# Empty-tile rows of a head's weighted sums added after the fourth key tile instead of after the sixth

## The chip, the cores and the metric

One Trainium2 chip, one core. The metric is device time in microseconds (us) of one execution. Engines: PE (TensorE, matmuls), DVE (VectorE), ACT (ScalarE), POOL (GpSimd), SP (SyncE, which here issues nearly all DMAs, in order).

## What is computed

Clustered attention over 2 batches x 8 heads of 768 tokens and 64 channels, and then two feed-forward layers on 1536 tokens of 512 channels. A query sees the keys of its own cluster only:

```python
q_assign = argmax(einsum('bhsd,hcd->bhsc', q_n, c_n)); k_assign = ...   # 16 clusters
mask = q_assign[:, :, :, None] == k_assign[:, :, None, :]
scores = np.where(mask, scale * (q @ k.T), -1e9)
attn = exp(scores - max); attn = attn / (sum(attn) + 1e-9)
x = (attn @ v)                                  # to [1536, 512]
h = x @ w_in;  x = softplus(h) @ w_out          # first layer, d_ff 2048
h = x @ w_in2; out = leaky_relu(h, 0.01) @ w_out2
```

A query whose cluster has no key gets equal scores everywhere, so its output is the mean of v. The kernel has a mend for this case: a few extra rows ("empty" rows) which are multiplied with sums over v and added to the head's weighted sums.

## The kernel before

The 16 heads (2 x 8) are worked through one after the other, overlapped. A head's 768 tokens are 6 tiles of 128 (C = 6). Line numbers are those of the profile.

For each head: q and k come in (L273, L274), are split into f16 high and low parts (L293 to L295) and transposed by a DMA (L297, tile t). 24 small matmuls (L306, tile as) and a few DVE operations give the cluster of each token (L319 to L325, tile oh); ACT writes these behind the channels of tile nq (L328, L329), and a second DMA transpose (L331) makes tile **tq** from nq. Then 12 score matmuls (L345) with a DVE maximum each (L352, tile mm) give the largest score of each query; DVE (L359, L361, tile dg), six small matmuls (L366) and ACT (L374) write these maxima, with the empty marks, into rows 96 to 127 of the same tile tq. Then for each of the six tiles of keys (kt = 0 to 5), emit_s2 makes scores (L392, L393, two banks), ACT takes exponentials (L399, tile p), POOL the low part (L401, tile pl), and emit_pv adds p times v to the head's sums in tile **x**, one PSUM bank: 6 matmuls each on L428, L429 and L433. In heads 0 to 7 one of the six key tiles is multiplied in f32 instead (L415) and has no pl. emit_sv makes the sums over v (L439, L440, DVE L445, tile svr). emit_empty, six matmuls on L451, multiplies rows 96 to 127 of tq with svr and adds them to x. emit_norm (DVE L470, L471, L473, ACT L475, POOL L476) reads x and normalises.

Tile tq has 4 buffers in heads 0 to 7 and 3 later: the transpose that fills the tq of head 15 can start when the last reader of the tq of head 12 is done, and likewise 14 behind 11 and 13 behind 10. The last reader of a tq in the program is emit_empty. Tile x has one buffer.

Beside the heads run the weights of the feed-forward layer: DMA loads (L153, tile st, two buffers), decoded by DVE (L140, L143, L146) and split by ACT and DVE (L162, L163). From head 8 on the first layer of the feed-forward fills in: groups of 12 matmuls (L697, one output tile each, read by ACT in L520, L521), later L710 with 48 per output tile; the first quarter of the tokens uses Abs, Relu, Exp, Ln on ACT, the others the softplus function of ACT's tables (L509, L510). After the heads come the rest of the first layer and the second layer (L562).

The order on each engine is not written out. The program emits steps with a priority (at_pri), and a list scheduler that simulates the machine places all of them; each engine then runs its list in order, with waits on semaphores where data or a buffer come from another engine. emit_s2 and emit_pv of key tile j of head h have priority h + j/6; the last emit_pv, and before the change emit_empty, have h + 1; a smaller number goes first.

Of the kernel before, what the change touches and what calls it, by code (L numbers as in the profile page):

```python
# [43 lines left out]

FF_PRI, FF_STEP, FF_RATE = 8, 0.25, 0.75

W_FREE, W_FROM, W_TO, W_PER = 4, 8, 10, 5
W_PRI = ((0, 0.5), (17, 0.3))
W2_STEPS = 88
# [7 lines left out]
def attn_moe_kernel(  # L57
# [13 lines left out]
    V, S, G, PE = nc.vector, nc.scalar, nc.gpsimd, nc.tensor  # L71
    B, H, SEQ, D = q.shape
    NCL = cen.shape[1]
    DM, DFF = w_in1.shape
    C = SEQ // 128
# [201 lines left out]
    def load_v(h):  # L277
        b, hh = divmod(h, H)
        vv = v32s[h % V_BUFS][:, :, 0:D]
        nc.sync.dma_start(out=vv, in_=v[b, hh].rearrange("(p c) d -> p c d", c=C))  # L280
        v_t[h] = vv

    def split_v(h):
        vv, v2 = v_t.pop(h), v2s[h % V_BUFS]
        S.copy(out=v2[:, :, D:2 * D], in_=vv)
        ENG[by_group(VLO, h)].tensor_tensor(out=v2[:, :, 0:D], in0=vv, in1=v2[:, :, D:2 * D], op=ALU.subtract)
# [50 lines left out]
    MR = 96  # L337
    KS2 = 128
# [15 lines left out]
    def emit_m(h):  # L354

        dg = dgs[h % len(dgs)]
        diag = dg.rearrange("p (c s) -> p c s", s=129)
        m = diag[:, :, MR:MR + 1]
        mark[h] = V.reduce_max(out=m, in_=mms[h % 2], axis=AX)  # L359
        empty = diag[:, :, MR + C:MR + 3 * C].rearrange("p c (t s) -> p c t s", s=C)[:, :, :, 0]  # L360
        V.tensor_scalar(out=empty, in0=m.to_broadcast([128, C, 2]), scalar1=-65504.0, scalar2=None, op0=ALU.is_equal)  # L361
        t = tp2[h][0]
        for j in range(2):
            bank = ring("s2", h)
            for c in range(3 * j, 3 * j + 3):
                PE.matmul(  # L366
                    out=bank[0:KS2, (c % 3) * 128:(c % 3 + 1) * 128],
                    lhsT=dg[:, c * 128:(c + 1) * 128],
                    rhs=ident,
                    start=True,  # L370
                    stop=True,
                )
            o = bank[MR:KS2, 0:3 * 128].rearrange("p (c r) -> p c r", c=3)
            S.copy(out=t[MR:KS2, 3 * j:3 * j + 3, :], in_=o)  # L374
        tpq[h] = t
# [28 lines left out]
    XW = D + 1  # L404

    def emit_pv(h, kt):
        v2 = v2s[h % V_BUFS]
        if kt == 0:
            x_t[h] = px.tile([128, 512], F32, tag="x", name="x")
        xps = x_t[h]  # L410
        p, pb, pl = p_t.pop((h, kt))
        if pl is None:
            pf = p.rearrange("p a r -> p (a r)")
            for c in range(C):
                PE.matmul(  # L415
                    out=xps[:, c * XW:(c + 1) * XW],
                    lhsT=pf[:, c * 128:(c + 1) * 128],
                    rhs=v32s[h % V_BUFS][:, kt, :],
                    start=(kt == 0 and c == 0),
                    stop=False,  # L420
                )
            return
        pb = pb.rearrange("p a r -> p (a r)")
        pl = pl.rearrange("p a r -> p (a r)")
        for c in range(C):
            cs = slice(c * 128, (c + 1) * 128)
            o = xps[:, c * XW:(c + 1) * XW]
            PE.matmul(out=o, lhsT=pb[:, cs], rhs=v2[:, kt, D:2 * D + 1], start=(kt == 0 and c == 0), stop=False)  # L428
            PE.matmul(out=o[:, 0:D], lhsT=pb[:, cs], rhs=v2[:, kt, 0:D], start=False, stop=False)  # L429
        for c in range(C):  # L430
            cs = slice(c * 128, (c + 1) * 128)
            o = xps[:, c * XW:(c + 1) * XW]
            PE.matmul(out=o, lhsT=pl[:, cs], rhs=v2[:, kt, D:2 * D + 1], start=False, stop=False)  # L433

    def emit_sv(h):
        v2 = v2s[h % V_BUFS]
        o = ring("as")[:, 0:XW]
        for kt in range(C):
            PE.matmul(out=o, lhsT=ones, rhs=v2[:, kt, D:2 * D + 1], start=(kt == 0), stop=False)  # L439
            PE.matmul(out=o[:, 0:D], lhsT=ones, rhs=v2[:, kt, 0:D], start=False, stop=(kt == C - 1))  # L440
        q4 = slice(MR, 128)
        h16 = atile([128, XW], F16, "h16", h)
        r = atile([128, XW], F16, "svr", h)
        S.copy(out=h16[q4], in_=o[q4])
        V.scalar_tensor_tensor(out=r[q4], in0=h16[q4], scalar=sel[q4], in1=o[q4], op0=ALU.mult, op1=ALU.add)  # L445
        svs[h] = r

    def emit_empty(h):
        t, r, xps = tpq[h], svs.pop(h), x_t[h]
        for c in range(C):  # L450
            PE.matmul(out=xps[:, c * XW:(c + 1) * XW], lhsT=t[MR:KS2, c, :], rhs=r[MR:KS2, :], start=False, stop=(c == C - 1))  # L451

    def emit_out(b, hh, xn):
        nc.sync.dma_start_transpose(
            out=xt[b][:, hh // 2].rearrange("p n (c r) -> p (n c) r", c=C), in_=xn.rearrange("p n c d -> p (n c d)")
        )
# [268 lines left out]
    def behind_tk(h):  # L725
        return tc.issue_after(tki[h].ins) if h in tki else nullcontext()

    @contextmanager
    def at_pri(x):
        old = tc.cur_priority  # L730
        tc.cur_priority = pri(x)
        yield
        tc.cur_priority = old
# [8 lines left out]
    with at_pri(-9):  # L742
# [6 lines left out]
            out=ss[:, 1:2], in0=ss[:, 0:1], scalar1=ss[:, 2:3], scalar2=ss[:, 1:2], op0=ALU.mult, op1=ALU.add  # L749
# [19 lines left out]
    for v2 in v2s:  # L769
# [3 lines left out]
        out=ident, in_=ones, pattern=[[1, 128]], compare_op=ALU.is_equal, fill=0.0, base=0, channel_multiplier=-1  # L773
# [4 lines left out]
    for j in range(NCL):  # L778
# [4 lines left out]
        out=sel, in_=sel, pattern=[[0, 1]], compare_op=ALU.is_ge, fill=0.0, base=-MR - 2 * C, channel_multiplier=1  # L783
# [9 lines left out]
    def w_step():  # L793
        w0, wr = W_PRI[cnt["w"] >= 34]
        with at_pri(w0 + wr * (cnt["w"] % 34)):
            if convs:
                n = cnt["w"] - 1
                g = -1 if n < W_FREE else int(W_FROM + (W_TO - W_FROM) * (n - W_FREE) / (32 - W_FREE))
                g = min(g, max(mark, default=-1), 15)
                bank = n < 2 * KDM * DFF // 512  # L800
                if g >= 0:
                    with tc.issue_after(mark[g].ins):
                        convs.pop(0)(bank)
                else:
                    convs.pop(0)(bank)
            if wq:
                with behind_tk(wtie["h"]):
                    convs.append(wq.pop(0)())
        cnt["w"] += 1
# [86 lines left out]
    def chain(h):  # L896
        if h < NH:
            with at_pri(h - LEAD_SPLIT):
                split(h)
            with at_pri(h - LEAD_ASSIGN):  # L900
                assign_mm(h)
                assign_el(h)
            with at_pri(h - LEAD_MAX):
                for c in range(C):
                    emit_s1(h, c)
            if h + 2 < NH:
                with at_pri(h - LEAD_LOAD):
                    load(h + 2)

    def moe_steps(n):  # L910
        st["credit"] += n
        while st["credit"] >= 1.0:
            with at_pri(FF_PRI + cnt["m"] * FF_STEP):
                next(ff, None)
            st["credit"] -= 1.0
# [5 lines left out]
    for h in range(NH):  # L921
        with at_pri(h - LEAD_M):
            emit_m(h)
        chain(h + AHEAD)
        wtie["h"] = h + 2
        with at_pri(h):
            if h + 1 < NH:
                split_v(h + 1)
            if h + 2 < NH:
                with behind_tk(h + 2):  # L930
                    load_v(h + 2)
            emit_sv(h)
            if h in outs_t:
                with behind_tk(h + 2):
                    emit_out(*outs_t.pop(h))
        for j in range(C):
            with at_pri(h + j / 6):
                emit_s2(h, j)
                if j:
                    emit_pv(h, j - 1)  # L940
            if h < H - 1 and (j + h * C) % W_PER == 0:
                w_step()
            if h > H or (h == H and j > 0):
                moe_steps(FF_RATE)
            if h == H and j == 0:
                open_late()
        with at_pri(h + 1):
            emit_pv(h, C - 1)
            emit_empty(h)
        with at_pri(h + 1 - LEAD_NORM):  # L950
            emit_norm(h)
    bctx.close()
# [48 lines left out]
```

## Time and profile before

| what | us |
|---|---|
| median of 3 runs | 734.06 (734.0 to 735.52) |
| profiled execution, its own time | 732.15 |
| its span, first to last instruction | 730.4 |
| PE busy in the span | 677.0 (93%) |
| DVE, ACT, POOL busy | 517.3, 410.9, 402.5 |

Heads run from about 12 us to 315 us of the span. From there to the end PE works through the feed-forward with hardly an idle moment. A reader should ask where PE is idle before 315 us, and which engine or queue ended each of these idle stretches. In timeline rows the columns are start, length, engine, line, operation, count, and in brackets the idle time of the engine just before with what ended it; matmuls overlap in their pipe, so the pace of PE is the distance between starts.

### The profile page before, as it was taken

To read this page: it belongs to the slowest core of one execution; us is meant where nothing else is said; L and a number is where in the kernel's file an instruction comes from. 1 tells how busy PE (TensorE), PEld (TensorE's weight loads), DVE (VectorE), ACT (ScalarE), POOL (GpSimd) and SP (SyncE) were. 2 spreads that over 40 slices of the span, in tenths; PEclk is the share of its full clock that TensorE was granted. 3 is DMA by queue.
4 is the path that set the end of the run, shared out by engine and by line. 5 is a ranking of instruction groups with operands and counts; after the bars stand their busy time and mean duration, and the time that the engine had idled before them with its cause. 6 is when DMAs were issued, how large, how long until landed. Compare 5 with 4: busy or idle time off the path is not lost. (4 is left out here: it accounts for less than half of the span.)

```text
span 730.4 us, 18968 instructions
## 1 busy us (share of the span) xinstructions
PE 677.0 (93%) x7584; PEld 506.7 (69%) x7584; DVE 517.3 (71%) x1167; ACT 410.9 (56%) x1087; POOL 402.5 (55%) x494
## 2 busy tenths in 40 slices
PE   1798899998889899999999999999999999999997
PEld 1367677665656566656666566558999999999996
DVE  4797798998898782069787867965585757575545
ACT  5476666768878753355245425526555555565553
POOL 6387777778888864303324233325556465565653
PEclk9999999999999999999999999999999999999999
DMA  8985966766565632013322355787000000000000
GB/s 204 221 173 113 181 136 122 170 123 173 129 161 152 141 116 53 2 35 103 110 93 82 108 175 193 235 304 261 3 31 2 30 2 7 27 2 31 2 31 30
DMA packets 104521, 77.87 MB, mean 107 GB/s; under 512 B 78320, under 2 KB 92656, under 8 KB 104432
## 3 DMA queue, kind: packets, MB, share of 16 engines
q1 hardware_dynamic: 104288, 76.40, 40.4%
q8 instruction: 59, 0.97, 0.5%
q14 instruction: 30, 0.25, 0.1%
q10 hardware_dynamic: 144, 0.26, 0.1%
HBM read 50.36 MB, written 10.49 MB: 83 GB/s over the span
## 5 line engine op out<-in xcount | busy, mean ns | idle before, releaser
L401 POOL TENSOR_TENSOR pl<-p 128x768 f16<-128x768 f32 x88 | 128.3, 1468 | 56.3 <-ACT p L399 36.0
L352 DVE TENSOR_REDUCE mm<-s 128x1 f32<-128x384 f32 x190 | 100.6, 548 | 19.3 <-PE s L345 16.7
L562 PEld LDWEIGHTS <-w_in2h 128*128 128x128 f16 x1344 | 98.2, 98 | 5.3 <-issue 0.7
L570 DVE TENSOR_TENSOR gl<-r,gh 128x384 f16<-128x384 f32 (+1 forms) x96 | 63.2, 659 | 50.0 <-ACT gh L608 49.3
L697 PE MATMUL m<-xt,w_inh 128*128 128x384 f16 x512 | 93.8, 326 | 4.2 <-ACT rl L521 3.4
L399 ACT ACTIVATE p<-s 128x384 f32<-128x384 f32 x160 | 74.2, 492 | 30.9 <-PE s L393 28.3
L710 PE MATMUL m<-g_l,w_outh 128*128 128x384 f16 x256 | 83.4, 326 | 2.0 <-DVE g_l L511 1.9
L710 PE MATMUL m<-g_h,w_outh 128*128 128x384 f16 x256 | 83.5, 326 | 0.0
L710 PE MATMUL m<-g_h,w_outl 128*128 128x384 f16 x256 | 83.3, 326 | 0.0
L570 POOL TENSOR_TENSOR r<-r,r 128x128 f32<-128x128 f32 x95 | 47.8, 520 | 55.5 <-ACT r L600 55.2
L697 PEld LDWEIGHTS <-w_inh 128*128 128x128 f16 x512 | 49.7, 98 | 38.7 <-issue 6.1
L608 ACT CAST gh<-r 128x384 f16<-128x384 f32 (+1 forms) x96 | 54.2, 565 | 36.6 <-POOL r L570 33.6
L710 PEld LDWEIGHTS <-w_outh 128*128 128x128 f16 x512 | 49.8, 98 | 32.5
L345 PE MATMUL s<-tq 128*128 128x384 f16 x190 | 62.0, 345 | 9.3 <-DMA tq<-nq 4.5
L562 PEld LDWEIGHTS <-gh 128*128 128x128 f16 x672 | 60.5, 98 | 6.4 <-issue 1.1
L200 POOL TENSOR_TENSOR wd<-wd 128x256 f32<-128x256 f32 x32 | 29.3, 925 | 53.9 <-DVE sg L194 39.2
L562 PE MATMUL i<-xt,w_in2h 128*128 128x128 f16 x576 | 57.2, 219 | 0.1
L392 PE MATMUL s<-t 128*128 128x384 f16 x160 | 53.2, 333 | 3.1 <-ACT p L399 2.3
L393 PE MATMUL s<-tq 128*128 128x384 f16 x160 | 53.2, 333 | 1.6 <-ACT tq L374 1.6
L562 PE MATMUL i<-sh,w_in2h 128*128 128x128 f16 x384 | 53.5, 219 | 0.4 <-ACT r L600 0.4
L562 PE MATMUL i<-sl,w_in2h 128*128 128x128 f16 x384 | 53.5, 219 | 0.0
L562 PE MATMUL i<-sh,w_in2l 128*128 128x128 f16 x384 | 53.4, 219 | 0.0
(145 smaller groups left out, 1861.1 us busy)
## 6 DMA issues: line engine op xcount, KB each, us to landing
st<-in_moe_w_in_dram SPq DMA_DIRECT2D x32, 512.0 KB, 4.6
st<-in_moe_w_out_dram SPq DMA_DIRECT2D x32, 512.0 KB, 3.7
kept<-sg SPq DMA_DIRECT2D x16, 256.0 KB, 2.8
qk<-in_q_dram SPq DMA_DIRECT2D x16, 192.0 KB, 3.5
qk<-in_k_dram SPq DMA_DIRECT2D x16, 192.0 KB, 3.7
v<-in_v_dram SPq DMA_DIRECT2D x16, 192.0 KB, 4.7
kept<-sg SPq DMA_DIRECT2D x24, 128.0 KB, 2.7
out_dram<-ob SPq DMA_DIRECT2D x11, 256.0 KB, 2.0
```

The lines of the kernel that those rows point to most:

```text
L200: G.tensor_tensor(out=out, in0=in0, in1=in1, op=ALU.subtract)
L345: PE.matmul(out=o, lhsT=t[:, c, :], rhs=tk[:, 3 * j:3 * j + 3, :], start=True, stop=True,)
L352: V.reduce_max(out=mms[h % 2][:, c, j:j + 1], in_=bank[:, 0:3 * 128], axis=AX)
L392: PE.matmul(out=o, lhsT=t1[:, kt, 1, :], rhs=t1[:, 3 * j:3 * j + 3, 0, :], start=True, stop=False)
L393: PE.matmul(out=o, lhsT=t2[:, kt, :], rhs=tqh[:, 3 * j:3 * j + 3, :], start=False, stop=True)
L399: S.activation(out=p[:, j, :], in_=sp, func=AF.Exp, scale=scale)
L401: G.tensor_tensor(out=pl, in0=p, in1=pb, op=ALU.subtract)
L562: one = PE.matmul(out=bank, lhsT=w_, rhs=x_, start=(first and i == 0), stop=(i == len(ops) - 1), skip_group_check=True)
L570: eng.tensor_tensor(out=out, in0=in0, in1=in1, op=op)
L608: S.copy(out=gh[:, lo:hi], in_=r[:, lo:hi])
L697: PE.matmul(out=hp, lhsT=w_, rhs=x_, start=(i == 0), stop=(i == len(ops) - 1))
L710: PE.matmul(out=yp, lhsT=w_[:, kk, ms], rhs=g_[:, kk, :], start=(n == 0), stop=(n == 3 * KFF - 1))
```

## The change

emit_empty is called behind emit_pv of key tile 3 (when j is 4), at priority h + 4/6, instead of behind emit_pv of key tile 5 at h + 1. The stop flag of the accumulation moves from the last empty matmul to the last matmul of emit_pv. No operation is added or removed in the source; since the scheduler places everything anew, the lists of all engines differ from the end of head 0 on.

```diff
+EMPTY_AT = 4
@@ emit_pv, f32 key tile
-                    stop=False,
+                    stop=(kt == C - 1 and c == C - 1),
@@ emit_pv, low parts
-            PE.matmul(out=o, lhsT=pl[:, cs], rhs=v2[:, kt, D:2 * D + 1], start=False, stop=False)
+            PE.matmul(
+                out=o, lhsT=pl[:, cs], rhs=v2[:, kt, D:2 * D + 1], start=False, stop=(kt == C - 1 and c == C - 1)
+            )
@@ emit_empty
-            PE.matmul(out=xps[:, c * XW:(c + 1) * XW], lhsT=t[MR:KS2, c, :], rhs=r[MR:KS2, :], start=False, stop=(c == C - 1))
+            PE.matmul(out=xps[:, c * XW:(c + 1) * XW], lhsT=t[MR:KS2, c, :], rhs=r[MR:KS2, :], start=False, stop=False)
@@ loop over heads
                 emit_s2(h, j)
                 if j:
                     emit_pv(h, j - 1)
+                if j == EMPTY_AT:
+                    emit_empty(h)
...
         with at_pri(h + 1):
             emit_pv(h, C - 1)
-            emit_empty(h)
```

Three places of the new order follow. In each the numbers behind a name tell buffers apart, and a line of "..." stands for matmuls of the same kind and for weight loads. After the change the lines stand one to three further down (L451 is L454, L433 is L434, L697 is L700).

**PE, from the empty rows of head 12 (x_4678, tq_3659) to the first score matmul of head 15 (s1_4942, on tq_4940).** Before:

```order
L433 MATMUL x_4678<-v2_0_89,pl_4824 128x65
...
L451 MATMUL x_4678<-svr_4641,tq_3659 128x65
...
L393 MATMUL s2_5113<-tq_4085 128x384
...
L697 MATMUL m_4365<-xt0_83,w_inh_79 128x384
...
L428 MATMUL x_5033<-v2_1_90,p_4999 128x65
...
L433 MATMUL x_5033<-v2_1_90,pl_5000 128x65
L345 LDWEIGHTS tq_4940
L345 MATMUL s1_4942<-tq_4940 128x384
```

After:

```order
L434 MATMUL x_4678<-v2_0_89,pl_4739 128x65
...
L454 MATMUL x_4678<-svr_4641,tq_3659 128x65
...
L429 MATMUL x_4678<-v2_0_89,p_4781 128x65
...
L394 MATMUL s2_5005<-tq_4085 128x384
...
L700 MATMUL m_4277<-xt0_83,w_inh_79 128x384
...
L394 MATMUL s2_5028<-tq_4085 128x384
...
L434 MATMUL x_4678<-v2_0_89,pl_4782 128x65
...
L429 MATMUL x_4678<-v2_0_89,p_4829 128x65
...
L346 MATMUL s1_4942<-tq_4940 128x384
```

The empty rows come two key tiles of head 12 earlier; between them and the score matmuls of head 15 stand, besides the empty rows, 4 score matmuls, 12 of L697, 12 of L428 and L429, and 5 of L433 before, and 8 score matmuls, 12 of L700, 24 of L429 and L430, and 6 of L434 after.

**PE, from the empty rows of head 11 (x_4199, tq_3204) to the first score matmul of head 14 (s1_4588, on tq_4586).** Before:

```order
L433 MATMUL x_4199<-v2_2_91,pl_4396 128x65
...
L451 MATMUL x_4199<-svr_4143,tq_3204 128x65
...
L393 MATMUL s2_4744<-tq_3659 128x384
...
L697 MATMUL m_4158<-xt0_83,w_inh_79 128x384
...
L428 MATMUL x_4678<-v2_0_89,p_4644 128x65
...
L345 MATMUL s1_4588<-tq_4586 128x384
```

After:

```order
L434 MATMUL x_4199<-v2_2_91,pl_4308 128x65
...
L454 MATMUL x_4199<-svr_4143,tq_3204 128x65
...
L429 MATMUL x_4199<-v2_2_91,p_4336 128x65
...
L394 MATMUL s2_4673<-tq_3659 128x384
...
L434 MATMUL x_4199<-v2_2_91,pl_4337 128x65
...
L429 MATMUL x_4199<-v2_2_91,p_4401 128x65
...
L442 MATMUL as_4981<-v2_1_90,ones_99 128x65
...
L346 MATMUL s1_4588<-tq_4586 128x384
```

Here the group of 12 feed-forward matmuls (L697) between the two is gone: there stand 4 score matmuls, 24 of L429 and L430, 6 of L434 and 12 of L442 and L443.

**ACT, at the last exponentials of head 15 and the first softplus (L509, L512 after).** Before:

```order
L399 ACTIVATE p<-s_5699 128x384
L714 ACTIVATE xt_83<-m 128x384
L399 ACTIVATE p<-s_5741 128x384
L399 ACTIVATE p<-s_5745 128x384
L509 ACT_TABLE_LOAD
L509 ACTIVATE g_h<-m 128x384
L510 ACTIVATE mr<-m 128x384
```

After:

```order
L400 ACTIVATE p<-s_5699 128x384
L512 ACT_TABLE_LOAD
L512 ACTIVATE g_h<-m 128x384
L513 ACTIVATE mr<-m 128x384
L400 ACT_TABLE_LOAD
L400 ACTIVATE p<-s_5747 128x384
L400 ACTIVATE p<-s_5751 128x384
L512 ACT_TABLE_LOAD
```

The last two exponentials now stand behind the first softplus, and two more table loads are in the list.

## Rows read from the trace of the kernel before

**Rows 1.** Page, busy time, share of the span and instructions of each engine.

```profile
PE 677.0 (93%) x7584; PEld 506.7 (69%) x7584; DVE 517.3 (71%) x1167; ACT 410.9 (56%) x1087; POOL 402.5 (55%) x494
```

**Rows 2.** Stretches: length, busy time of each engine, granted clock, DMA share, GB/s.

```profile
core 0: us, PE busy (x) PEld busy (x) DVE busy (x) ACT busy (x) POOL busy (x), PEclk, DMA share, GB/s
...
30.00:50.00 20.00, 18.01 (x197) 12.32 (x196) 16.29 (x37) 14.49 (x36) 12.68 (x11) 1.00 1.04 231
50.00:165.00 115.00, 105.36 (x1573) 78.48 (x1571) 99.13 (x238) 77.78 (x192) 86.59 (x73) 1.00 0.68 137
165.00:250.00 85.00, 73.92 (x910) 49.26 (x908) 72.92 (x150) 70.16 (x173) 72.36 (x65) 1.00 0.61 149
```

**Rows 3.** Waits of PE, 35 to 320 us: total us, times, longest.

```profile
PE s L345 <- DVE mm L352: 3.9, 9, 0.9
PE m L697 <- ACT rl L521: 3.4, 8, 0.7
...
PE s L345 <- DMA tq<-nq: 2.3, 2, 1.9
```

**Rows 4.** Waits of the SP queue, 30 to 250 us.

```profile
SPq L331 <- PE x L451: 28.2, 8, 8.0
SPq L153 <- DVE wcp L146: 21.2, 7, 5.6
```

**Rows 5.** Timeline, PE, head 11's empty rows to head 14's scores.

```profile
225.41 0.35 PE L433 MATMUL x<-v,pl 128*128 128x65 f16 x6
225.69 0.35 PE L451 MATMUL x<-svr,tq 32*128 32x65 f16 x6
225.98 0.34 PE L392 MATMUL s<-t 128*128 128x384 f16 x1
...
226.48 0.33 PE L393 MATMUL s<-tq 128*128 128x384 f16 x1
227.43 1.46 PE L697 MATMUL m<-xt,w_inh 128*128 128x384 f16 x8 [0.63 <-ACT rl L521]
...
229.38 0.19 PE L428 MATMUL x<-v,p 128*128 128x65 f16 x1
...
229.86 0.50 PE L345 MATMUL s<-tq 128*128 128x384 f16 x2
```

**Rows 6.** Timeline, SP queue, the last two transposes into tq and what follows.

```profile
226.08 1.42 SPq L331 DMA_TRANSPOSE tq<-nq  x1
...
228.59 14.27 SPq L153 DMA_DIRECT2D st<-in_moe_w_out_dram  x4
244.72 1.46 SPq L331 DMA_TRANSPOSE tq<-nq  x1
```

**Rows 7.** Line L331: from issue to landing.

```profile
DMA to landing us min/median/max: 3.6/3.9/5.4
```

**Rows 8.** Timeline, PE, head 12's empty rows and head 15's first scores.

```profile
244.29 0.35 PE L451 MATMUL x<-svr,tq 32*128 32x65 f16 x6
...
250.18 0.50 PE L345 MATMUL s<-tq 128*128 128x384 f16 x2 [1.92 <-DMA tq<-nq]
```

**Rows 9.** Stretches around that wait.

```profile
248.27:250.18 1.91, 0.00 (x0) 0.00 (x0) 0.54 (x1) 0.81 (x2) 0.95 (x2) 1.00 1.28 84
...
250.70:254.10 3.40, 3.40 (x39) 2.37 (x36) 1.66 (x4) 2.27 (x6) 3.24 (x3) 0.50 0.88 238
```

**Rows 10.** Timeline, PE, the two next longest idle times after 30 us.

```profile
33.10 0.48 PE L393 MATMUL m<-tq 128*128 128x384 f16 x1 [1.73 <-ACT tq L374]
...
61.34 0.32 PE L393 MATMUL s<-tq 128*128 128x384 f16 x1 [1.40 <-ACT tq L374]
```

**Rows 11.** Timeline, DVE and PE, around 167 to 172 us.

```profile
166.97 0.69 DVE L140 TENSOR_SCALAR wcp<-st 128x512 int32<-128x512 int32 x1 [1.68 <-DMA st<-in_moe_w_in_dram]
...
170.34 0.32 PE L345 MATMUL s<-tq 128*128 128x384 f16 x1 [0.75 <-DVE mm L352]
171.25 0.32 PE L345 MATMUL s<-tq 128*128 128x384 f16 x1 [0.59 <-DVE mm L352]
```

**Rows 12.** Timeline, ACT, last exponential and first softplus.

```profile
308.48 0.49 ACT L399 ACTIVATE p<-s 128x384 f32<-128x384 f32 x1 [1.45 <-PE s L393]
308.99 1.28 ACT L509 ACT_TABLE_LOAD   x1
310.29 0.49 ACT L509 ACTIVATE g_h<-m 128x384 f16<-128x384 f32 x1
310.67 0.48 ACT L510 ACTIVATE mr<-m 128x384 f32<-128x384 f32 x1
```

**Rows 13.** Page, costliest groups: POOL's low parts (busy, mean ns, idle before).

```profile
L401 POOL TENSOR_TENSOR pl<-p 128x768 f16<-128x768 f32 x88 | 128.3, 1468 | 56.3 <-ACT p L399 36.0
```

## Prediction, made before the changed kernel ran

> **What bounds the kernel now.** I read the page's busy shares first: PE is busy for 677.0 us of a 730.4 us span, far ahead of DVE [rows 1]. From 315 us on, past the heads, the feed-forward keeps PE busy, so a microsecond that PE idles while the heads run is a microsecond at the end. The stretches show how much there is: PE lacks 115.00 - 105.36 = 9.6 us between 50 and 165 us, and 85.00 - 73.92 = 11.1 us between 165 and 250 us [rows 2]. PE's matmuls stay the same 7584, so the change can only move these idle microseconds, and the time at a lower clock.
>
> The waits of PE name many small causes, none over 4 us in all [rows 3]. The longest single one after 30 us is 1.92 us at 250.18, on the transpose into tq [rows 8]. The SP queue tells where that comes from: L331 stood 28.2 us, in 8 waits, behind the empty rows L451, the last reader of the tq whose buffer it fills [rows 4]. Head 15 shows the chain: L451 at 244.29, the transpose issued at 244.72, the score matmul at 250.18 [rows 6, 8]. So the empty rows matter little as work and much as the release of a buffer.
>
> **What the change does, part by part.**
>
> *The empty rows themselves.* Six take 225.98 - 225.69 = 0.29 us of PE [rows 5]. They are moved, not removed: 0 for PE. They no longer stand between the last low parts and the norm, but the norm waits in DVE's list anyway; I count nothing there, and at most 16 x 0.29 = 4.6 us if every head's end stood on PE's path, which the waits contradict: none of PE's larger ones is on x [rows 3].
>
> *Release of tq.* The new order puts the empty rows two key tiles earlier, and the last score matmuls on that tq (key tile 5) stand before them, so the release does move. But the scheduler has moved the readers of the next tq forward too, so what counts is the PE work between release and reader. Paces from the rows: 0.29 for six empty rows, 0.66 for four score matmuls (225.98 to 226.48 is three), 12 of L697 in 229.38 - 227.43 = 1.95, 12 of L428 and L429 in 0.38 to 0.48 (229.38 to 229.86), six of L433 in 0.28 [rows 5]; the 12 sums over v cost about as much as 12 of L428 and L429. The need, from the start of the empty rows to the reader, is 0.4 to issue [rows 5, 6] plus 3.9 median, 5.4 at most [rows 7]: 4.3, or 5.9.
>
> - Head 15: before, 0.29 + 0.66 + 1.95 + 0.38 + 0.2 = 3.5 us of work against 5.9 in reality; waited 1.92, the rest were small gaps. After, 0.29 + 0.38 + 0.66 + 1.95 + 0.66 + 0.28 + 0.38 = 4.6 us: the wait falls to 5.9 - 4.6 = 1.3, or to none at the median landing. I take the middle, 0.65: a gain of **1.3**. Behind the 1.92 us of idle time, PE ran at half its granted clock, 1.2 instead of 2.4 GHz, for 3.40 us of solid matmuls [rows 9]; that cost 1.7 us. Idle times of 1.73 and 1.40 us [rows 10] were not followed by a lower clock: it reads 1.00 in both stretches [rows 2]. So a wait of 0.65 gives the **1.7** back. Together -3.0, bounds -3.6 (no wait) and -0.6 (wait of 1.3 and the clock falls all the same).
> - Head 13: 0.3 us of wait, the other one of the two [rows 3], goes: after, 4.8 us of work by the same count. **-0.3**.
> - Head 14: before, the reader came 229.86 - 225.69 = 4.17 after the empty rows [rows 5], at the landing. In the new order the group of 12 feed-forward matmuls is gone from between: 0.29 + 0.38 + 0.66 + 0.28 + 0.38 + 0.38 = 2.4 us of work. The wait is 4.2 - 2.4 = 1.8 us, and nothing stands before the reader that PE could do instead. **+1.7**, bounds 0 (other waits fill it) and +3.5 (1.8 and a clock fall; 1.8 lies between the 1.73 that was not followed by one and the 1.92 that was; nearer to 1.73, so I count none).
> - Heads 4 to 10 have 15 us and more of PE work between release and reader in either order: 0.
>
> *The feed-forward groups.* A group of L697 waits for ACT to read the bank of the group before. PE's waits on this are 3.4 us in 8 [rows 3]. Before the one of 0.63 [rows 5] some 2.9 us of work stood between two groups, so 3.5 was needed there. In the new order this pair has only six low parts, 4 score matmuls and 3 of L346 between it, 0.28 + 0.66 + 3 x 0.163 = 1.4 us: a wait of 2.1 if ACT is as laden with exponentials as before, and of 0.63 if it is not. I take the middle, 1.4, in place of 0.63: **+0.7**, bounds 0 and +2.0 with another pair that comes closer.
>
> *What stands behind L331 in the SP queue.* Loads of weights follow it. One arrived late at 166.97 and held DVE for 1.68 us, and PE then waited 0.75 and 0.59 us for maxima [rows 11]. An earlier release lets that load go earlier: **-0.7**, half of the 1.34, bounds -1.34 and 0.
>
> *ACT's two extra table loads.* The first softplus now stands before the last two exponentials. ACT needs 1.28 + 0.38 + 0.48 [rows 12], another 1.28 and 0.87 for the exponentials, 4.3 us from the group's end, then POOL 1.47 for the low part [rows 13]: 5.8. PE has 5.2 us of work in its list until it needs that (20 of L697, 4 score matmuls, empty rows, 24 of L429 and L430, 12 of L434). **+0.7**, bounds 0 and 2.6 (both loads in full).
>
> The page "ScalarE: Activation LUTs" of the Trainium skill (What ACT_TABLE_LOAD costs) puts a switch of set at about 2.66 us with the drain, twice the load. In the trace the load ends at 310.27 and the next operation starts at 310.29 after an exponential that ended 0.02 before the load [rows 12], so no drain is seen and the measurement decides. By the page this term would be +3.4 and the whole +1.8.
>
> **Sum.** -3.0 - 0.3 + 1.7 + 0.7 - 0.7 + 0.7 = -0.9 us on the profiled execution's own 732.15 (span 730.4 and 1.75 around it): 731.2. The median of the runs stands 1.9 above the profiled one, so 734.06 - 0.9 = **733.1**.
>
> **The rivals.**
>
> 1. *Faster: the SP queue was the brake.* If the 28.2 us of waiting in the queue [rows 4] held more than those two readers, then score maxima, exponentials and weights all come earlier, and PE's waits on mm and tq shrink too: 3.9 on mm [rows 3] and the 1.40 [rows 10]. Half of these, 2.6, and head 14's 1.7 filled by them: -0.9 - 2.6 - 1.7 = -5.2, 728.9; with half of that 731. For it: the sheer size of the queue's wait. Against: an earlier reader was put into the list at once, so the slack is spent already.
>
> 2. *Slower: the loads ahead of the transpose take the release's place.* Before L331 of head 15 stand four weight loads, which left between 228.59 and 242.86, each held until DVE had decoded an earlier one [rows 4]; L331 itself left at 244.72 [rows 6]. If the release comes some 5 us earlier, at 239.5, the fourth load at 242.9 holds the transpose. Then the reader waits 242.9 + 3.9 less 239.2 + 4.6, 3.0 us, and the clock falls: +1.1 and 0 in place of -1.3 and -1.7, in all +3.2, 737.3. With head 14's wait drawing a clock fall as well it is 739. It decides at whether DVE's decode before that load ends earlier than the empty rows of head 12. In the new list this decode stands before the maxima's step (L359) of head 14, and PE's matmuls on that (L366) before the empty rows of head 12, so I think it does, barely.
>
> 3. *No effect: the release isn't early in time*, since the fourth key tile's low parts come late from POOL (1.47 us each [rows 13]) and the scheduler spends what it gains. Then only the reshuffle remains, within 1 us either way: 733 to 735.
>
> All lists differ from the end of head 0 on, and the small waits, some 18 us in all, are dealt anew; I allow 2 us either way for that around every case.
>
> **How the numbers follow.** The forecast with rival 3: 0.37 to come out within 0.2% (1.5 us, about what a measurement of this kernel can tell from no change). Rival 1, and the forecast's own better end: faster by more, 0.36. Rival 2, head 14's clock fall, or the extra tables and groups at their upper bounds: slower by more, 0.27. The range reaches from rival 1 at 729.5 to rival 2 at 738.0; below and above I leave one in ten each. The likeliest case's own range is 732 to 735.5.
>
> **What would show it.** Right: the transposes of heads 13 to 15 leave the SP queue at L454 of heads 10 to 12 and two key tiles before the heads' ends; an idle PE of 1 to 2 us before head 14's first L346; under 1.3 us before head 15's; clock 1.00 there; three table loads about the last exponentials with less than 1 us of PE idle. Wrong: PE idle in 50 to 250 us below 16 us or above 24 (20.7 now [rows 2]); the release of head 15's tq at a weight load instead of L454; a second stretch at half clock.

## The result, and the profile after

The changed kernel takes **739.38 us** (median of 7 runs, 736.42 to 742.18) against 734.06 (7 runs, 732.03 to 737.14) of the kernel before on the same chip: a ratio of 1.0073, interval 1.0050 to 1.0096. It is slower; I had forecast 733.1 and a range up to 738.0. The profiled execution took 740.92, its span is 739.2.

Lines of after are those of before plus 1 for the scores (L345 is L346), plus 3 from the sums over v on (L439 is L442, L451 is L454, L697 is L700). The page, busy times as in [rows 1], and its row of the granted clock in 40 slices:

```profile
PE 684.1 (93%) x7584; PEld 510.1 (69%) x7584; DVE 517.2 (70%) x1167; ACT 414.3 (56%) x1089; POOL 402.2 (54%) x494
...
PEclk9998999999998999999999999999999999999999
```

PE is busy for 7.1 us more with the same 7584 matmuls, and idle for 55.1 us against 53.4. Most of the difference of the two profiled executions is therefore slower matmuls, not waiting. The stretches of [rows 2], and four short ones in which the clock is at its lower level (1.2 instead of 2.4 GHz); columns as in [rows 2]:

```profile
50.00:165.00 115.00, 103.92 (x1485) 77.52 (x1483) 95.77 (x223) 74.50 (x186) 83.06 (x68) 0.96 0.63 135
165.00:250.00 85.00, 76.90 (x920) 50.64 (x919) 70.54 (x155) 67.26 (x165) 68.37 (x62) 0.94 0.58 133
```

```profile
56.60:63.40 6.80, 6.80 (x75) 6.29 (x71) 3.14 (x8) 3.80 (x9) 4.25 (x5) 0.50 0.80 196
152.20:155.60 3.40, 3.21 (x50) 2.87 (x50) 3.40 (x10) 1.38 (x3) 2.64 (x3) 0.50 0.61 179
206.80:210.20 3.40, 3.40 (x17) 1.70 (x14) 3.19 (x8) 2.04 (x6) 1.99 (x2) 0.50 1.04 204
230.70:237.50 6.80, 6.01 (x19) 2.87 (x20) 2.89 (x6) 3.41 (x8) 0.99 (x1) 0.50 0.62 184
```

These four are 20.4 us long; behind its start before had one of 3.4 [rows 9]. The other 17 us at half speed are worth 8.5 at most, about the difference of the two spans, 8.8. But this split belongs to the two profiles and not to the kernels: e4 below has after's order on PE and the same time, yet its profile has only 10.2 us at the lower level behind the start, and PE idle for 57.2 us. How much of the 5 us the clock holds, and how much idle time, stays open. Nor can the granted clocks of all runs settle it, since they miss the start: in both kernels PE begins at the lower level (a score matmul takes 0.48 to 0.53 us instead of 0.33) and leaves it only at about 39 us in before and 36 us in after, where the granted clock reads 1.00 all the time. The last section shows this.

Three places that the prediction spoke of. First head 14's start on PE, which answers [rows 5]: the feed-forward group between empty rows and scores is gone, and two pauses stand there, with slow matmuls (0.53 instead of 0.33 us) behind them. Then the SP queue, which answers [rows 6], and head 15's first scores, which answer [rows 8]:

```profile
226.31 0.35 PE L454 MATMUL x<-svr,tq 32*128 32x65 f16 x6
...
229.59 0.19 PE L442 MATMUL as<-v,ones 128*128 128x65 f16 x1 [1.26 <-DVE oh L326]
...
231.49 0.82 PE L346 MATMUL s<-tq 128*128 128x384 f16 x2 [1.37 <-DMA tq<-nq]
232.10 0.53 PE L393 MATMUL s<-t 128*128 128x384 f16 x1
```

```profile
226.69 1.43 SPq L332 DMA_TRANSPOSE tq<-nq  x1
228.17 0.89 SPq L281 DMA_DIRECT2D v<-in_v_dram  x1
229.17 19.72 SPq L154 DMA_DIRECT2D st<-in_moe_w_out_dram  x4
249.00 2.48 SPq L332 DMA_TRANSPOSE tq<-nq  x1
```

```profile
248.11 0.35 PE L454 MATMUL x<-svr,tq 32*128 32x65 f16 x6
...
254.11 0.50 PE L346 MATMUL s<-tq 128*128 128x384 f16 x2 [0.67 <-DMA tq<-nq]
```

The waits of PE (35 to 320 us) and of the SP queue (30 to 250 us), as in [rows 3, 4]:

```profile
PE as L307 <- DMA t<-n: 4.7, 5, 1.6
PE s L346 <- DVE mm L353: 3.9, 5, 1.3
...
PE s L346 <- DMA tq<-nq: 2.2, 3, 1.4
...
PE m L700 <- ACT rl L524: 1.8, 4, 0.5
```

```profile
SPq L154 <- DVE wcp L147: 39.0, 10, 8.0
...
SPq L332 <- PE x L454: 4.0, 3, 1.6
```

The transposes' wait on the empty rows fell from 28.2 us to 4.0, as the change means it to. Yet PE waits for tq as long as before, 2.2 us against 2.3. That is the riddle. What grew is PE's wait on the transpose of k (tile t); before had

```profile
PE as L306 <- DMA t<-n: 2.8, 4, 1.2
```

### The profile page after: what moved, and what is told of

Read it like the earlier page. It is cut to its first block, busy times and chain, and to the rows that moved or that the text cites. A ratio compares the mean times of both kernels' runs of the same rounds, so it can differ in the third digit from the quotient of the medians.

```text
span 739.2 us, 18973 instructions
## 1 busy us (share of the span) xinstructions
PE 684.1 (93%) x7584; PEld 510.1 (69%) x7584; DVE 517.2 (70%) x1167; ACT 414.3 (56%) x1089; POOL 402.2 (54%) x494
## 5 line engine op out<-in xcount | busy, mean ns | idle before, releaser
L700 PE MATMUL m<-xt,w_inh 128*128 128x384 f16 x512 | 97.0, 332 | 3.0 <-ACT rl L524 1.8
L700 PEld LDWEIGHTS <-w_inh 128*128 128x128 f16 x512 | 50.3, 99 | 37.4 <-issue 5.3
L346 PE MATMUL s<-tq 128*128 128x384 f16 x190 | 62.8, 348 | 9.9 <-DMA tq<-nq 4.8
L565 PE MATMUL i<-xt,w_in2h 128*128 128x128 f16 x576 | 57.2, 219 | 0.1
L565 PE MATMUL i<-sh,w_in2l 128*128 128x128 f16 x384 | 53.4, 219 | 0.0
```

Of the source, the lines that this page charges most:

```text
L346: PE.matmul(out=o, lhsT=t[:, c, :], rhs=tk[:, 3 * j:3 * j + 3, :], start=True, stop=True,)
L565: one = PE.matmul(out=bank, lhsT=w_, rhs=x_, start=(first and i == 0), stop=(i == len(ops) - 1), skip_group_check=True)
L700: PE.matmul(out=hp, lhsT=w_, rhs=x_, start=(i == 0), stop=(i == len(ops) - 1))
```

## The experiments

Theory **deal**: the early place is a gain, and what the scheduler makes of it, new lists on every engine, loses more. Rival **place**: the early release itself brings things forward that collide. Further rivals: a single spot (head 14's group, the table loads), the order in the SP queue, or noise of any new deal.

Most kernels below are the changed kernel with the order of every engine given. A helper ties each instruction to the one that is to stand ahead of it on its engine, by an edge that orders without a semaphore; the lists of numbers (ORDER) are the order of before, that of after, or a mix. It adds no instruction:

```diff
     moe2(tp, ctx.enter_context(tc.tile_pool(name="pt", bufs=1)))
+    impose(nc, tc)
...
+            if prev is not None:
+                tc.add_manual_dep(
+                    written[at],
+                    prev.name,
+                    mybir.DependencyInfo(mybir.DependencyClass.NoSync, mybir.DependencyReason.DATA),
+                    reason="order",
+                )
```

All results in one table. "Cover" is the PE work in its list between the release of a tq buffer and the first score matmul on the tile that takes it, for heads 12 to 15, with each matmul counted at its start-to-start distance at full clock (0.163 us for 384 columns, 0.030 to 0.034 for 64 and 65). "tq waits" is what PE waited for the DMA into tq between 35 and 320 us of the profiled execution. The ratio is to runs of before in the same comparison.

| kernel | ratio, 95% interval | cover, us | tq waits, us |
|---|---|---|---|
| before | 1 | 3.5, 3.0, 3.0, 3.2 | 2.3 |
| after | 1.0073 (1.0050 to 1.0096) | 4.0, 4.3, 2.0, 4.2 | 2.2 |
| e1 old lists, early rows | 0.9903 (0.9875 to 0.9931) | 9.2, 8.6, 9.1, 7.9 | 0 |
| e3 group ahead | 1.0079 (1.0053 to 1.0105) | 4.0, 4.3, 4.0, 4.2 | 0.8 |
| e4 one table | 1.0063 (1.0039 to 1.0088) | as after | 2.4 |
| e5 behind fifth | 1.0011 (0.9986 to 1.0037) | 4.3, 2.3, 3.6, 3.9 | 2.6 |
| e6 new from head 8 | 1.0038 (1.0016 to 1.0060) | as after | 2.2 |
| e7 new to head 8 | 0.9937 (0.9916 to 0.9958) | as e1 | 0 |
| e8 early in head 12 alone | 0.9973 (0.9953 to 0.9994) | 3.5, 3.0, 3.0, 7.9 | 0.3 |
| e9 new order on SP alone | 1.0005 (0.9980 to 1.0030) | as e1 | 0 |
| e10 new from head 12 | 1.0043 (1.0022 to 1.0064) | as after | 4.6 |
| e11 behind third, new deal | 1.0068 (1.0044 to 1.0092) | 6.2, 4.2, 5.4, 2.2 | 2.1 |
| e12 new deal, nothing moved | 0.9995 (0.9977 to 1.0014) | as before | 2.3 |
| e13 behind third, old lists | 0.9928 (0.9904 to 0.9952) | 9.7, 10.8, 10.7, 10.3 | 0 |
| e14 planned as if late | 1.0005 (0.9983 to 1.0027) | 8.8, 7.8, 8.9, 7.7 | 0 |
| e15 the same, third | 0.9995 (0.9976 to 1.0014) | 10.5, 10.7, 10.7, 9.3 | 0.2 |
| e16 the same, 14 and 15 only | 1.0066 (1.0042 to 1.0090) | 4.0, 4.3, 7.4, 8.2 | 0.4 |

**e1: the place without the deal.** The lists of before; only the six empty rows of each head stand where the change puts them.

> All engines keep the lists of the kernel before, word for word (each list is imposed by order edges); only the six empty-row matmuls of each head stand, on PE, right behind the low parts of key tile 3, as the change asks for. Theory R (the change is slow because the scheduler dealt all lists anew, and the new lists make PE pause so that its clock falls): as fast as before or faster, 730 to 734.5 us, no more half clock than the 3.4 us of before; the transposes into tq of heads 13 to 15 leave earlier and the wait of 1.92 us before head 15 shrinks. Theory E (the early place of the empty rows itself costs, by the earlier transposes colliding with loads or by waits in PE's list): slower than before, 737 to 741 us.

728.79 us: 1.0% under before, 1.7% under the changed kernel, from one and the same source. Page and stretches:

```profile
PE 674.6 (93%) x7584; PEld 505.0 (69%) x7584; DVE 518.2 (71%) x1167; ACT 410.2 (56%) x1087; POOL 401.5 (55%) x494
...
PEclk9999999999999999999999999999999999999999
```

```profile
50.00:165.00 115.00, 105.16 (x1544) 77.74 (x1543) 99.03 (x235) 77.97 (x193) 86.29 (x72) 1.00 0.73 145
165.00:250.00 85.00, 77.08 (x980) 52.01 (x979) 77.08 (x160) 72.03 (x179) 75.68 (x69) 1.00 0.67 149
```

Between 165 and 250 us PE does 77.08 us of work at full clock, where before did 73.92 [rows 2] and after 76.90 partly at half speed. So "place" falls, and the early release is worth about 7 us (0.97% of 734; 5 to 9 by the interval). The two profiles show only a part of it: their spans differ by 2.5 us, and between 50 and 250 us PE lacks 17.8 us instead of 20.7. In SP's queue the weight loads hold the last transpose here too, and it doesn't matter:

```profile
224.76 15.62 SPq L154 DMA_DIRECT2D st<-in_moe_w_out_dram  x4
240.47 1.66 SPq L332 DMA_TRANSPOSE tq<-nq  x1
```

Head 12's empty rows ran from 236.77 to 237.12, the transpose left 3.4 us after that behind the fourth load, and head 15's first scores came at 245.64 without a wait: the cover of 7.9 us was enough.

**e3 and e4: single spots.** e3 is the changed kernel's order with one feed-forward group (12 matmuls of L700) put back between empty rows and scores of head 14; e4 is that order with the last two exponentials ahead of the first softplus on ScalarE, so that one table load is left of three.

> The changed kernel with its own lists, except that one group of 12 feed-forward matmuls (the eleventh of L700) is moved ahead of the sums over v (L442, L443) that stand before head 14's first score matmul. Theory R, with the pause there (1.26 and 1.37 us of idle PE, then 6.8 us at half clock) as its largest part: 3 to 5.5 us faster than the changed kernel, 734 to 736.5 us, and no half clock at 230 us. If the half clock comes from elsewhere, or the pauses only move: within 1.5 us of the changed kernel, 738 to 741 us.

> The changed kernel with its own lists, except that on ACT the last two exponentials stand ahead of the first softplus, so that only one table load is left there. If the extra loads are what it costs: 737 us or less, 2 us or more under the changed kernel. If they are nearly hidden: 0 to 1.5 us under it, 738 to 739.5 us.

Neither moved the time: 1.0079 and 1.0063 against 1.0073. e3 is a miss that the timeline explains: the group put ahead has to wait itself, longer than the two pauses it was to fill.

```profile
230.66 1.46 PE L700 MATMUL m<-xt,w_inh 128*128 128x384 f16 x8 [3.10 <-ACT rl L524]
```

So e3 shows that a filler can't be had there, not that the pause is free. For the tables, e4's difference of 0.1% is within the intervals. Both kernels also show that an imposed order costs nothing by itself: they are the lists of after with one change each, and take its time.

**e5: another place, dealt anew.**

```diff
-EMPTY_AT = 4
+EMPTY_AT = 5
```

> The change with EMPTY_AT = 5: the empty rows come behind key tile 4, with all lists dealt anew by the scheduler. Theory R: its time has no order with the place; it lies anywhere from 731 to 742 us, and follows the microseconds of half clock and of idle PE in its own trace. Theory E: between the kernel before and the changed one, 735 to 738 us.

735.6, no difference from before. With e11 below, every new deal with earlier rows is as slow as before or slower.

**e6, e7, e10: which stretch.** Up to the first score matmul of a head the order of one kernel, from there that of the other; the empty rows stand early throughout.

> The empty rows stand early in all heads. Every engine follows the order of before up to the first transpose of head 8 (about 130 us) and the changed kernel's order from there to the end. Kernel before in the last comparison: 734.8 us; the order of before with early rows: 728.8; changed kernel: 739.4. Theory 'loss in many places' (the newly dealt order costs something in every stretch; of the changed kernel's half-clock time 6.8 us lie in the first half and 13.7 in the second): 735 to 737, with half clock left only behind 150 us. Theory 'late heads' (all of it is made by the order around heads 12 to 14, where feed-forward groups and the weight loads were moved): 738.5 to 740. Theory 'early heads' (a delay made early is carried to the end): 729 to 731.

> The counterpart: every engine follows the changed kernel's order up to the first transpose of head 8, and the order of before, with the empty rows early, from there on. 'Loss in many places': 731.5 to 734, the two halves' losses together making up the 10.6 us between 728.8 and 739.4. 'Late heads': 728 to 730. 'Early heads': 737.5 to 740.

> The empty rows early in all heads; the order of before up to the first transpose of head 12 (about 195 us) and the changed kernel's order from there. With the new order from head 8 on the time was 737.7, with the old order alone 728.8. Theory 'head 14' (the two pauses of 2.6 us ahead of head 14 with the slow matmuls behind them, 4.5 us of lag in the changed kernel's trace, and the 1.4 us of table loads at 320 us make most of it): 733.5 to 736. Theory 'heads 8 to 11' (the pauses around 147 to 152 us): 729 to 731.

The medians are 737.70 for e6, which lies between the ranges of its theories, 730.17 for e7, just above "late heads", and 735.94 for e10, inside "head 14", which e16 below doesn't bear out. Against e1's 0.9903, the new order costs 0.34% in heads 0 to 7 (e7), 1.35% from head 8 on (e6) and 1.40% from head 12 on (e10), each with some 0.35 either way. The two halves add up to 1.69%, and the whole loss is 1.70%. Heads 8 to 11 cost nothing that can be measured, and about four fifths of the loss lie from head 12 on. PE's longest group of waits in e10:

```profile
PE s L346 <- DMA tq<-nq: 4.6, 3, 2.9
```

**e9: SP's order alone.** All engines in the old order, SyncE in the new. One piece of the difference on SP (transposes of k's tile t and of tq, loads of q and k):

```diff
 L275 DMA qk<-in_k_dram 128x384
+L298 DMA_TRANSPOSE t_3167<-n_3160 128x12x128
 L332 DMA_TRANSPOSE tq<-nq_85 128x12x128
...
-L298 DMA_TRANSPOSE t_3167<-n_3160 128x12x128
```

> The empty rows early, the order of before on TensorE, VectorE, ScalarE and GpSimd, and the changed kernel's order on SyncE alone, that is, its order of DMA issues. Theory 'DMA order' (transposes of q queued behind weight loads make the pauses): 735 or more. Theory 'order on TensorE' (the loads come early enough in either order; what the changed kernel lost, it lost by the order of its matmuls): 728 to 730.

734.29, ratio 1.0005: 1.0% slower than e1, just short of the 735 of "DMA order". The timelines show one swap that makes a large part of it: SP in e1, SP in e9, then ScalarE and PE in e9.

```profile
135.92 1.80 SPq L332 DMA_TRANSPOSE tq<-nq  x1
...
139.09 3.78 SPq L298 DMA_TRANSPOSE t<-n  x1
```

```profile
140.07 1.44 SPq L298 DMA_TRANSPOSE t<-n  x1
141.61 1.78 SPq L332 DMA_TRANSPOSE tq<-nq  x1
```

```profile
145.74 0.51 ACT L294 CAST nq<-qk 128x384 f16<-128x384 f32 x1 [5.00 <-DMA tq<-nq]
147.21 0.32 PE L393 MATMUL s<-t 128*128 128x384 f16 x1 [4.02 <-ACT tq L375]
```

L298 is held in the queue until 140.07, and L332 behind it leaves 5.7 us later than in e1; ScalarE waits 5.00 us for the transpose to have read nq, and the copy into tq behind that holds PE for 4.02. The changed kernel has the same order on SP, but there the same copy on ScalarE waits only 0.39 us (at 144.42); its other lists were dealt together with it. So this is no piece of its loss; it shows how little slack a list has when another one changes.

**e8: head 15's term by itself.** The old lists, with the rows early in head 12 alone:

```diff
-                if j == EMPTY_AT:
+                if j == EMPTY_AT and h in EARLY:
                     emit_empty(h)
...
             emit_pv(h, C - 1)
+            if h not in EARLY:
+                emit_empty(h)
```

> The order of before on every engine; only head 12, whose tile the transpose of head 15 waits for, has its empty rows behind the fourth key tile, and the other 15 heads keep them at the end. The prediction's terms for head 15 (its 1.9 us wait gone or shorter, the half clock behind it gone) give 734.8 - 3.0 = 731.8. Theory 'every head gains a little': 734 to 735. Theory 'all of the 6 us gained with the old order comes from head 15': 728.5 to 729.5.

731.82, ratio 0.9973: a gain of 2.0 us (0.4 to 3.4). The prediction's 3.0 for head 15 holds within the interval; the rest of e1's gain comes from the other heads.

**e11 and e12: is any new deal slow?** e11 puts the rows behind the third tile and lets all lists be dealt; e12 is the kernel before with one constant a little off.

```diff
-FF_PRI, FF_STEP, FF_RATE = 8, 0.25, 0.75
+FF_PRI, FF_STEP, FF_RATE = 8, 0.25, 0.76
```

> The empty rows one key tile earlier than in the change (behind the low parts of the third tile), with no order imposed: all lists are dealt anew once more. Theory 'place' (the time follows from how early the rows stand, and the changed kernel's loss belongs to an early place): 739 or more. Theory 'deal' (the loss belongs to the lists that happened to come out): anything from 729 to 742, and no rank by place among behind the fifth (735.6), the fourth (739.4) and the third.

> The kernel before with the rows at the end, and one constant of the planner a little off (FF_RATE 0.76 for 0.75), which deals part of the lists anew and moves nothing else. Theory 'deal' (a new deal alone moves the time by more than 0.3%): at least 2.2 us away from 734, on either side. Theory 'a deal averages out', which the prediction's 2 us either way stood for: 733 to 735.5.

e11 is slow again (737.73), e12 is not (733.04). e12 is a weak control, a single deal whose first score matmuls stand where they stood, so it doesn't show how far a new deal alone can move the time. What is shown: three deals with earlier rows give 1.0011, 1.0073 and 1.0068, three more below (e14 to e16) 1.0005, 0.9995 and 1.0066, and none of the six comes near the 0.99 of the old order.

**e13: still earlier, old lists.** The rows behind the third tile, order of before.

> The order of before on every engine, with the empty rows behind the third tile of keys instead of the fourth. Theory 'release': the last other reader of the tile, the last score product of the head, now sets when the tile comes free, so little more is gained: 727.5 to 729.5, against 728.8 behind the fourth. Theory 'the earlier the better': under 727. Theory 'too early' (the rows wait for their sums on VectorE): over 730.

727.72, ratio 0.9928: the same as e1 within the intervals. A cover of 8 us is enough, 10 gives nothing more.

**e14 to e16: the planner told of the old release.** The table's cover column names the suspect. The scheduler, which simulates the machine, sees tq come free earlier and pulls the score matmuls of heads 12 to 15 ahead by 5.2, 3.5, 5.8 and 4.0 us of PE work, so the cover stays at 2.0 to 4.3 us although the release stands about 5 us of work earlier. In e14 the scheduler alone, by an edge without a semaphore, takes the transpose to depend on the last weighted sum of the head that holds the buffer. The chip may still start it early.

```diff
+        if h in HOLDER:
+            tc.add_manual_dep(
+                tki[h].ins,
+                ended[HOLDER[h]].name,
+                mybir.DependencyInfo(mybir.DependencyClass.NoSync, mybir.DependencyReason.DATA),
+                reason="planner",
+            )
...
             emit_pv(h, C - 1)
+            ended[h] = nc.cur_bb.bb.instructions[-1]
```

HOLDER names the head that holds the buffer (15 behind 12, 14 behind 11, and so on); e15 is the same with EMPTY_AT = 3, e16 has HOLDER for heads 14 and 15 only.

> The changed kernel, its lists dealt by the planner as there; the one difference is that the planner, and not the chip, takes the transpose of q of a head to depend on the last weighted-sum matmul of the head that holds its buffer, as if the empty rows still stood at the end. In the lists that come out the first score product of heads 12 to 15 stands 8.8, 7.8, 8.9 and 7.7 us of matmul behind the release of its buffer (in the changed kernel 4.0, 4.3, 2.0 and 4.2; in the kernel before 3.5, 3.0, 3.0 and 3.2). Theory 'pulled ahead' (the planner, told of the earlier release, moves the score products and the weight loads ahead by as much, and the pauses come from that): 729 to 732, at least 7 us under the changed kernel. Theory 'other lists' (the loss is in the order of everything else that was dealt anew): 735 to 740.

> The same with the empty rows behind the third tile (737.7 without it): the first score products of heads 12 to 15 stand 10.5, 10.7, 10.7 and 9.3 us behind the release (without it 6.2, 4.2, 5.4 and 2.2). 'Pulled ahead': 728 to 731.5. 'Other lists': 735 to 739.

> The same as the first of these, for heads 14 and 15 alone (7.4 and 8.2 us; heads 12 and 13 keep the changed kernel's 4.0 and 4.3). 'Pulled ahead', with the loss mostly at head 14 (4.5 us of the changed kernel's lag): 733.5 to 735.5. With the loss mostly at heads 12 and 13: 736.5 to 739.

e14 came out at 1.0005 against 1.0073, e15 at 0.9995 against 1.0068: in both places the hint gives back 0.7% (5 us), and the waits on tq are gone. e16 gives back nothing that can be measured (739.48, above both its ranges), although head 14's wait on tq and the lower clock behind it are gone there: that spot, the most visible in the changed kernel's trace, doesn't decide the time by itself. What e14 has over e16 are the hints for heads 4 to 13, with 12 and 13 among them.

The hint is thus worth two fifths to a half of the loss. By which waits, isn't shown, since all lists are dealt anew with it. The waits on tq alone don't rank the kernels: e3 and e16 with 0.8 and 0.4 us are as slow as after with 2.2, and e5 with 2.6 is as fast as e14 with none. e14 and e15 fell short of e1 and e13 by 1.0% and 0.7%, which neither forecast of mine named: they missed the range of "pulled ahead" by 2.8 and 1.4 us. What that other half is, stays open; e4 speaks against the tables, and e9 shows that a single swap in a list can hold PE for 4 us. One lead that no run tests: PE's waits on the transposes of k are 3.9 to 5.6 us in the eight kernels whose lists were all dealt anew with the rows early (after, e3 to e5, e11, e14 to e16), and 2.8 to 3.5 in those with the old lists or nearly so (before, e1, e8, e12, e13); e6, slow with 3.0, speaks against it. PE's largest waits in e14 (lines 8 higher than in after) are many small ones:

```profile
PE s L354 <- DVE mm L361: 4.8, 9, 1.5
PE as L308 <- DMA t<-n: 4.8, 5, 1.6
```

Not tried: the changed kernel's lists with the rows at the heads' end (their scores stand 2.0 to 4.3 us of work behind the release, which would then come some 5 us later, behind its own readers, so that neither could go on), and a fourth late buffer for tq.

## Why the prediction was wrong

**What failed is the last step, the lists.** "All lists differ from the end of head 0 on ... I allow 2 us either way." The lists cost 1.7% (12 us) against the same source in the old order. I had taken the new deal as noise around the terms, and counted cover only where I looked, at heads 13 to 15. But this scheduler, told of an earlier release, uses it: it moved the score matmuls of heads 12 to 15 ahead by 3.5 to 5.8 us of work. Rival 1's "against", that the slack is spent already, was right for the lists and should have been the forecast. That the time then rises, and not only stays, had no term, and only rival 2 a price, by another cause; a part of it (0.7%) is undone when the scheduler isn't told (e14, e15), the rest is open. Without the deal rival 1's number comes out, -5.2 us beside e1's -7.1 (5 to 9), but not by its working: PE's waits on mm fell from 3.9 us only to 3.5.

**The clock step failed with it.** I let a pause cost clock only from some 1.9 us on, because 1.73 and 1.40 had not [rows 10]. The 1.73 was misread: the matmul behind it takes 0.48 us, against 0.32 behind the 1.40, so PE stood at 1.2 GHz there, although the granted clock of that stretch reads 1.00 [rows 2]. And in after the clock reads 0.50 behind shorter ones: 0.61 us ahead of the stretch at 56.6; 1.33 and 1.09 ahead of that at 152.2; 0.55 and 0.58 ahead of that at 206.8; 1.26 ahead of that at 230.7, and 1.37 across its start.

```profile
55.50 0.79 PE L346 MATMUL s<-tq 128*128 128x384 f16 x2 [0.61 <-DVE mm L353]
```

```profile
149.19 0.32 PE L346 MATMUL s<-tq 128*128 128x384 f16 x1 [1.33 <-DVE mm L353]
151.66 0.32 PE L346 MATMUL s<-tq 128*128 128x384 f16 x1 [1.09 <-DVE mm L353]
```

Term by term:

- *Head 15*, -3.0: right. No lower clock there, and e8 gives 2.0 (0.4 to 3.4) for it alone. That 0.67 us of wait stand beside 0.65 is luck: 0.65 was the middle between 0 and 1.3.
- *Head 14*, +1.7 with bounds to +3.5: right in place, too small. The wait on tq is 1.37 (1.8 by the working); the pause of 1.26 before it, on DVE, had no term, and 6.01 us of slow matmuls cost 3.0: 5.6 in the trace. e16 shows that its repair alone brings nothing.
- *Head 13*, -0.3: right. The wait of 0.4 us before its scores is gone.
- *Feed-forward groups*, +0.7: wrong in sign. The waits on rl fell from 3.4 us to 1.8.
- *Loads behind L331*, -0.7: didn't come. Their wait on the decode grew from 21.2 us [rows 4] to 39.0, and PE's waits on mm stayed at 3.9.
- *Table loads*, +0.7: the trace has the two extra loads and 1.9 us of idle PE between 300 and 330 us against 0.6, but e4, with one load, has 2.05 there and the same time. So no run shows a cost of the loads; and by the prediction's own paces the work in the list was 5.5 us rather than 5.2. The drain that the Trainium skill's page "ScalarE: Activation LUTs" (What ACT_TABLE_LOAD costs) adds to a load isn't seen in any of the three; the load at 317.18 ends at 318.46, and the exponential starts at 318.48:

```profile
317.18 1.28 ACT L400 ACT_TABLE_LOAD   x1
318.48 0.87 ACT L400 ACTIVATE p<-s 128x384 f32<-128x384 f32 x2
```

- *Rival 2*, weight loads ahead of the transpose: seen (249.00, right behind the fourth load), but head 12's empty rows ran only at 248.11, so it held the transpose by half a microsecond. In e1 it holds it by 3.4 us and costs nothing. Right side, wrong cause.
- *What would show it*: of the signs of being wrong two came, the last transpose released at a weight load, and a second stretch at half clock (there are four). PE's idle time between 50 and 250 us, the third, stayed inside its bounds at 19.2 us.

## What to carry to other kernels

Where a scheduler deals the lists, an earlier release is first of all an input to the scheduler: compare, list against list, how much work stands between a release and its reader, before pricing any wait. Try such a change with the old order held fixed as well; here that is the better kernel, 1.0% under the one before (e1; e13 is its equal), and it tells the gain of the edit from the cost of the deal. A term like "the rest is reshuffled, 2 us either way" needs a measured spread; here it had a direction too, for all six deals with earlier rows came out slower than the old order.

## What the runs showed of the hardware

In after the clock fell to 1.2 GHz behind groups of pauses of which none was over 1.4 us, in one case of 0.55 and 0.58, while a pause of 1.40 us left it at 2.4 [rows 10, 61.34]. And where it falls isn't fixed by the order: e4 has the changed kernel's order on PE and the same pause of 0.61 us ahead of this stretch (at 55.25), but its clock stays at 2.4 GHz where after's was at 1.2:

```profile
56.60:63.40 6.80, 5.94 (x109) 5.08 (x106) 3.67 (x9) 4.45 (x11) 4.77 (x5) 1.00 0.85 200
```

Its own falls come at 151.2, 205.8 and 417.5 us, 3.4 us each. A profile is one draw of these falls.

The granted clock of a profile isn't complete either. The same stretch in before and in e12:

```profile
28.25:38.49 10.24, 7.94 (x70) 4.91 (x70) 7.62 (x19) 5.55 (x16) 4.00 (x4) 1.00 1.03 207
28.25:38.49 10.24, 7.89 (x70) 4.91 (x70) 7.67 (x20) 5.49 (x16) 4.08 (x4) 0.50 1.00 215
```

Both run 70 matmuls in the same time, and in both one of 384 columns takes about 0.5 us, as at 1.2 GHz (0.48 at 33.10 in [rows 10]); only e12's record says so. In all 17 profiles the first score matmuls, from about 20 us on, run at this pace, and no record shows it. So the length of the matmuls has to be read beside the granted clock, and the mean clocks of two runs can differ by 0.7% (10.24 us at half, of 730) without a difference in pace.
